# One weight load issued earlier at the start, one addition moved from VectorE to ScalarE and GpSimd at the end

## The chip, the cores and the metric

The kernel runs on one core of a Trainium2 chip. The metric is device time in microseconds (us), from launch to the last byte of the output; lower is better. A profile of one execution stands beside it, and its span is the time between the first and the last instruction that the profiler saw.

## What is computed

Four sequences of 768 rows with 8 heads of width 64 go through a linear attention with decay, and the result, laid out as 3072 rows of 512, through a two-layer network with a residual. In the reference, cut to what matters (blocks of 64 rows, `lam` one decay factor per head):

```
intra = (qb @ kb.T * Dmask) @ vb                 # Dmask: lam ** (i - j), lower triangle
inter = (qb * lam_pow) @ kv_state
out   = intra + inter
kv_state = lam ** 64 * kv_state + (kb * rev_pow).T @ vb
...
xn = (x - mean) / sqrt(var + 1e-6) * g_ln        # x: 512 wide, all heads of a row
y  = x + relu(xn @ w_ch1) @ w_ch2                # w_ch1: 512 x 2048, w_ch2: 2048 x 512
```

## The kernel before, in words

The rows are cut into 12 windows of 256 rows, numbered u = 0 to 11; window u belongs to sequence u mod 4, and in a window each of the 128 partitions holds two rows. For every window the three inputs q, k and v are loaded (f32, 512 KB each), brought to bf16 with powers of the decay multiplied in (`in_k`, `in_q`, `in_v`), k and q are transposed, and TensorE does the scores, the products with v, the state, and the part that comes from the state. The result is normalised (`norm`), transposed again (`to_xT`) and passed through the network (`mlp(g)`, one group g for each window). The first product of the network takes W1 in four pieces, `w1[0]` to `w1[3]`, the second W2 in four pieces. Windows 0 and 1 take the second product as it stands (`m2`), the groups from 4 on do it with seven half-size products (`m2w`, P1 to P7) that are combined by `evict`.

Nothing is left to a scheduler. The program is one list of calls, each engine executes its own instructions in the order in which they stand in the list, and an engine whose next instruction waits stands still with all that is behind it. Five queues matter here.

- **SP** issues the loads of q, k and v. Window 0 is loaded in two halves of four heads (`load_window(0, parts=2)`, line 126, in the order k, q, k, q, v, v), then k and q of window 1 (lines 756 and 757); v of window 1 is issued late, behind a memset on VectorE (lines 785 and 786).
- **GpSimd (POOL)** makes the constants, casts the second half of window 0's k (`in_k(0, nc.gpsimd, HB)`, line 768), issues the pieces of W1 and W2 (`load_w1`, `load_w2`; these transfers change f32 to bf16 or f16 on the way), multiplies v (`in_v`), and takes half of window 1's q (line 977).
- **VectorE (DVE)** takes the first half of k and all of q of window 0, later the other half of window 1's q (line 978), the masks and the normalisations.
- **ScalarE (ACT)** computes the powers of the decay (`lam_q`, line 185), copies out the transposes, casts all of window 1's k (line 972), and applies the activation behind the first product.
- **TensorE (PE)** follows the list: transposes of window 1's k, the transposes of window 0's first half of normalised rows, the transposes of window 1's q (lines 999 and 1000), the first tile of the first product (`m1a.tile(0, 0)`, line 1001, needs `w1[0]`), the scores of window 1, the second tile (`m1a.tile(0, 1)`, line 1010), and then the product with `w1[1]` (line 1011).

A transfer is held back with `behind(x)`: GpSimd copies one column of x into a spare tile, so that it waits for x, and all that it issues later waits with it.

```
743  def behind(tile_ap):
745      nc.gpsimd.tensor_copy(seen_p, tile_ap)
975  behind(st[1]["kq"][:, 0, 0, 0, 0, 0:1])
976  load_w1(1)
979  behind(w1[0][:, 0, 0:1])
980  load_w1(2)
981  load_w1(3)
```

In this way `w1[1]` is issued when ScalarE has cast window 1's k, and the last two pieces when `w1[0]` has landed.

At the end of the last group the seven products come in the order P1, P2, P7, P5, P6, P4, P3. P1 and P6 go to PSUM tile a, P2 to b, P7 and P4 to c, P5 and P3 to d. `evict(i)` adds a finished product to the rows of x, times the factor of the row. For P1 and P7 ScalarE multiplies and GpSimd adds; for the others VectorE does both in one instruction (`scaled`, line 595). P6 is used twice: for both halves of the second 128 rows (one instruction of 128x512) and for the second half of the first 128 rows (one of 128x256). As soon as a quarter of the output is complete, `last_rows` has it stored, half by SP and half by ScalarE (line 636).

Of the kernel before, what the change touches and what calls it, by code (L numbers as in the profile page):

```python
# [11 lines left out]
ALU = mybir.AluOpType  # L12
ACT = mybir.ActivationFunctionType
# [4 lines left out]
def kernel(  # L18
# [11 lines left out]
    nc = tc.nc  # L30
# [4 lines left out]
    NU = B * S // W  # L35
# [80 lines left out]
    def load_w1(c):  # L116
        nc.gpsimd.dma_start(w1[c], moe_w_ch1[:, c * W1C:(c + 1) * W1C].rearrange("(k p) f -> p k f", p=128))
# [66 lines left out]
    lam_q = const.tile([128, H, 2], F32)  # L184
# [20 lines left out]
    def part(a, dst, hs):  # L205

        return dst[:, a, hs.start // 2:hs.stop // 2].rearrange("p a j e d -> p a e j d")
# [3 lines left out]
    def in_k(u, eng, hs=ALL):  # L211
        src = qkv_in[u]["k"][:, hs].rearrange("p (a e) j d -> p a e j d", e=2)
        dst = part(0, st[u]["kq"], hs)
        for j in range(2):
            (eng.copy if eng is nc.scalar else eng.tensor_copy)(dst[:, :, :, j], src[:, :, :, j])

    def in_q(u, eng, hs=ALL):
        src = qkv_in[u]["q"][:, hs].rearrange("p (a e) j d -> p a e j d", e=2)
        dst = part(1, st[u]["kq"], hs)
        if u < LB:  # L220
            lq = lam_q[:, hs, :].rearrange("p (a e) j -> p a e j", e=2)
        else:
            lq = lam_p[:, 0:1, hs].rearrange("p j (a e) -> p a e j", e=2).to_broadcast([128, (hs.stop - hs.start) // 2, 2, 2])
        n = (hs.stop - hs.start) // 2
        for j in range(2):
            eng.tensor_tensor(dst[:, :, :, j], src[:, :, :, j],
                              lq[:, :, :, j:j + 1].to_broadcast([128, n, 2, D]), op=ALU.mult)
# [304 lines left out]
    def mlp(g):  # L532
# [36 lines left out]
        pr = {}  # L569
# [15 lines left out]
        ev = {}  # L585

        def evict(i):
            u = g
            x, rstd = x_keep[u]
            w = DM // 2  # L590
            r = [rstd[:, ab:ab + 1] for ab in range(2)]
            xq = [[x[:, ab, z * w:(z + 1) * w] for z in range(2)] for ab in range(2)]

            def scaled(out, in0, ab, in1):
                nc.vector.scalar_tensor_tensor(out, in0=in0, scalar=r[ab], in1=in1, op0=ALU.mult, op1=ALU.add)  # L595

            def tmp(name):
                ev[name] = wk.tile([128, w], F32, tag="ev_" + name, bufs=1, name="ev_" + name)
                return ev[name]

            if i == "P1":
                o_of[u] = x
            o = o_of[u]
            oq = [[o[:, ab, z * w:(z + 1) * w] for z in range(2)] for ab in range(2)]
            if i == "P1":
                nc.scalar.activation(tmp("u1"), pr["a"], ACT.Identity, scale=r[0])  # L606
                nc.gpsimd.tensor_tensor(oq[0][0], ev["u1"], xq[0][0], op=ALU.add)  # L607
            elif i == "P2":
                scaled(oq[0][0], pr["b"], 0, oq[0][0])
                if u == NU - 1:  # L610
                    for j in range(2):
                        nc.sync.dma_start(rows_of(u)[j][:, 0, 0:w], o[half[j], 0, 0:w])
            elif i == "P7":
                nc.scalar.activation(tmp("p7"), pr["c"], ACT.Identity, scale=r[1])
                nc.gpsimd.tensor_tensor(xq[1][1], ev["p7"], xq[1][1], op=ALU.add)  # L615
            elif i == "P5":
                scaled(xq[1][1], pr["d"], 1, xq[1][1])
            elif i == "P6":
                scaled(o[:, 1].rearrange("p (z w) -> p z w", z=2), pr["a"][:, None, :].to_broadcast([128, 2, w]), 1,
                       x[:, 1].rearrange("p (z w) -> p z w", z=2))  # L620
                last_rows(1, 1)
                scaled(oq[0][1], pr["a"], 0, xq[0][1])
            elif i == "P4":
                scaled(oq[1][0], pr["c"], 1, oq[1][0])
                last_rows(1, 0)
            elif i == "P3":
                scaled(oq[0][1], pr["d"], 0, oq[0][1])
                last_rows(0, 1)

        def last_rows(ab, z):  # L630
            u = g
            if u < NU - 1:
                return
            sl = slice(z * (DM // 2), (z + 1) * (DM // 2))
            for j, eng in enumerate((nc.sync, nc.scalar)):
                eng.dma_start(rows_of(u)[j][:, ab, sl], o_of[u][half[j], ab, sl])
# [7 lines left out]
        def m2w(n):  # L644
            for q, r in order[7 * n:7 * n + 7]:
                i, bank, first = products[q]
                product(i, bank, [r], first and r == 0)
                if r == 7:
                    evict(i)
# [44 lines left out]
    def rows_of(u):  # L694

        cc, b = divmod(u, B)
        order = "(c p j) d -> j p c d" if u < LB else "(j c p) d -> j p c d"
        return out[b, cc * W:(cc + 1) * W, :].rearrange(order, c=2, j=2)
# [43 lines left out]
    def behind(tile_ap):  # L742

        seen_p = wk.tile([128, 1], F32, tag="seen_p", name="seen_p")
        nc.gpsimd.tensor_copy(seen_p, tile_ap)
# [19 lines left out]
    nc.vector.tensor_copy(e_p[:, 0:1], io_p)  # L765
    nc.vector.tensor_scalar(e_p[:, 1:2], e_p[:, 0:1], -1.0, None, op0=ALU.mult)
    in_q(0, nc.vector, HA)
    in_k(0, nc.gpsimd, HB)
    load_w1(0)
    in_q(0, nc.vector, HB)  # L770
    transpose_pe(0, 1, (0, 1))
    transpose_pe(0, 0, (2, 3), nc.vector)
# [618 lines left out]
```

## Time and profile before

| | |
|---|---|
| median of three runs | 208.27 us (207.52 to 208.6) |
| the profiled execution's own time | 207.48 us |
| its span | 205.7 us |
| PE busy | 195.9 us, 95% |
| DVE, ACT, POOL busy | 133.4, 122.0, 83.9 us |
| granted TensorE clock | 1.0 |

The profiled execution is 0.79 us below the median, and 1.78 us of its own time lie outside the span. PE is busy nearly throughout; the profile's own page warns that a busy PE is not PE at its peak, but here it means that little idle time is left to win: the idle time of PE lies at the start, before 21 us, and after its last product at the end.

### The profile page before, as it was taken

To read this page: it belongs to the slowest core of one execution; us is meant where nothing else is said; L and a number is where in the kernel's file an instruction comes from. 1 tells how busy PE (TensorE), PEld (TensorE's weight loads), DVE (VectorE), ACT (ScalarE), POOL (GpSimd) and SP (SyncE) were. 2 spreads that over 40 slices of the span, in tenths; PEclk is the share of its full clock that TensorE was granted. 3 is DMA by queue.
4 is the path that set the end of the run, shared out by engine and by line. 5 is a ranking of instruction groups with operands and counts; after the bars stand their busy time and mean duration, and the time that the engine had idled before them with its cause. 6 is when DMAs were issued, how large, how long until landed. Compare 5 with 4: busy or idle time off the path is not lost.

```text
span 205.7 us, 7488 instructions
## 1 busy us (share of the span) xinstructions
PE 195.9 (95%) x3223; PEld 157.8 (77%) x3223; DVE 133.4 (65%) x277; ACT 122.0 (59%) x281; POOL 83.9 (41%) x117
## 2 busy tenths in 40 slices
PE   1997999999999999999999999999999999999992
PEld 0485798545784686489889888888888888988881
DVE  3588352626766458777889774857877947865253
ACT  3787678535357468166575775585586565652630
POOL 5557039317656341464273261772273202002020
PEclk9999999999999999999999999999999999999999
DMA  3999999999899998999799999887988020178404
GB/s 105 301 255 203 179 281 192 198 293 277 194 268 252 217 183 190 170 256 213 165 201 134 220 213 135 207 169 128 234 133 183 4 51 3 26 131 273 139 7 97
DMA packets 91011, 36.41 MB, mean 177 GB/s; under 512 B 65121, under 2 KB 88161, under 8 KB 90978
## 3 DMA queue, kind: packets, MB, share of 16 engines
q1 hardware_dynamic: 86368, 31.53, 74.9%
q0 software_dynamic: 4224, 4.19, 12.7%
q8 instruction: 25, 0.41, 0.9%
q10 hardware_dynamic: 386, 0.20, 0.4%
q14 instruction: 8, 0.07, 0.1%
HBM read 27.27 MB, written 6.29 MB: 163 GB/s over the span
## 4 chain that ended last, share of the span: by engine, by line
PE 85%; DMA 6%; DVE 2%; ACT 2%; SPq 1%; issue 1%; POOL 0%; POOLq 0%; DVEq 0%
PE pm L547 34%; PE pm L684 14%; PE pm1t L658 6%; PE pwd L582 6%; PE pwa L582 6%; PE pwc L582 6%; DMA w<-in_moe_w_ch_dram 4%; PE pwb L582 3%; DMA qin<-in_q_dram 3%; PE po L449 2%; PE po L436 2%; DVE x L595 1%; PE po L423 1%; PE sc L370 1%; PE sc L279 1%; PE pk L324 1%
## 5 line engine op out<-in xcount | busy, mean ns | idle before, releaser
L547 PE MATMUL pm<-xT,w 128*128 128x256 bf16 x640 | 73.9, 273 | 0.4 <-DMA w<-in_moe_w_ch_dram 0.4
L547 PEld LDWEIGHTS <-w 128*128 128x128 bf16 x640 | 61.2, 98 | 8.7 <-DMA w<-in_moe_w_ch_dram 0.5
L550 ACT ACTIVATE hT<-pm 128x512 f16<-128x512 f32 x80 | 47.1, 597 | 28.7 <-PE pm L547 28.5
L684 PE MATMUL pm<-w,hT 128*128 128x512 f16 x128 | 29.8, 380 | 0.0
L582 PEld LDWEIGHTS <-hs 128*128 128x128 f16 x256 | 24.9, 98 | 2.9
L607 POOL TENSOR_TENSOR x<-ev_u,x 128x256 f32<-128x256 f32 x8 | 5.9, 743 | 48.8 <-ACT ev_u L606 37.4
L330 POOL TENSOR_TENSOR Sn<-Stmp,lam_s 128x256 bf16<-128x256 f32 x16 | 9.8, 616 | 33.0 <-DVE Stmp L408 17.9
L565 DVE TENSOR_TENSOR hs<-hT 128x1024 f16<-128x1024 f16 x16 | 12.7, 795 | 15.8 <-ACT hT L550 14.5
L684 PEld LDWEIGHTS <-hT 128*128 128x128 f16 x128 | 11.8, 98 | 12.4
L582 PEld LDWEIGHTS <-hT 128*128 128x128 f16 x192 | 18.7, 98 | 2.1
L658 PE MATMUL pm1t<-xT,w 128*128 128x128 bf16 x256 | 15.6, 219 | 1.0 <-DMA w<-in_moe_w_ch_dram 0.7
L477 DVE SCALAR_TENSOR_TENSOR xc<-po,nmean,g_row 128x512 bf16<-128x512 f32 x18 | 13.0, 745 | 5.0 <-ACT nmean L476 4.9
L658 PEld LDWEIGHTS <-w 128*128 128x128 bf16 x256 | 14.8, 98 | 1.5 <-DMA w<-in_moe_w_ch_dram 0.8
L475 ACT ACTIVATE x<-po 128x512 f32<-128x512 f32 x18 | 10.6, 590 | 7.8 <-PE po L449 4.5
L242 POOL TENSOR_TENSOR vb<-vin,lam_v 128x1024 bf16<-128x1024 f32 (+1 forms) x7 | 11.6, 1659 | 4.8 <-DMA vin<-in_v_dram 4.7
L520 ACT ACTIVATE sq<-x,nmean 128x512 bf16<-128x512 f32 x18 | 12.9, 719 | 0.3
L242 POOL TENSOR_TENSOR vb<-vin,lam_p 128x1024 bf16<-128x1024 f32 x6 | 11.4, 1896 | 3.1 <-ACT hT L550 1.9
L289 DVE TENSOR_TENSOR mA<-sc,keep 128x512 bf16<-128x512 f32 x14 | 9.0, 682 | 4.9 <-PE sc L279 4.9
L661 ACT ACTIVATE hT<-pm1t 128x512 f16<-128x512 f32 x16 | 9.6, 598 | 4.4 <-PE pm1t L658 4.3
L595 DVE SCALAR_TENSOR_TENSOR x<-pwd,rstd,x 128x256 f32<-128x256 f32 x16 | 7.7, 481 | 3.4 <-POOL x L615 3.4
L595 DVE SCALAR_TENSOR_TENSOR x<-pwa,rstd,x 128x512 f32<-128x512 f32 (+1 forms) x16 | 9.1, 612 | 0.8
L582 PE MATMUL pwa<-w,hT 128*128 128x256 f16 x64 | 9.6, 273 | 0.0
(137 smaller groups left out, 318.0 us busy)
## 6 DMA issues: line engine op xcount, KB each, us to landing
out_dram<-x SPq DMA_DIRECT2D x22, 256.0 KB, 4.0
w<-in_moe_w_ch_dram POOLq DMA_DIRECT2D x8, 512.0 KB, 8.0
kin<-in_k_dram SPq DMA_DIRECT2D x14, 256.0 KB, 5.2
qin<-in_q_dram SPq DMA_DIRECT2D x14, 256.0 KB, 4.2
vin<-in_v_dram SPq DMA_DIRECT2D x14, 256.0 KB, 5.3
kin<-in_k_dram SPq DMA_DIRECT2D x5, 512.0 KB, 6.2
qin<-in_q_dram SPq DMA_DIRECT2D x5, 512.0 KB, 7.0
vin<-in_v_dram SPq DMA_DIRECT2D x5, 512.0 KB, 6.1
```

Source lines behind the costliest of these rows:

```text
L242: eng.tensor_tensor(st[u]["vb"][:, hs], qkv_in[u]["v"][:, hs], lv.to_broadcast([128, n, 2, D]), op=ALU.mult)
L330: eng.tensor_tensor(dst, src, lam_s[:, :, None].to_broadcast([128, NP, D]), op=ALU.mult)
L475: nc.scalar.activation(x, po, ACT.Copy, accum_out=sm)
L477: nc.vector.scalar_tensor_tensor(xc, in0=po, scalar=nm, in1=g_row, op0=ALU.add, op1=ALU.mult)
L520: nc.scalar.activation(sq, s["x"][:, ab], ACT.Square, bias=s["nmean"][:, ab:ab + 1], accum_out=ss[:, ab:ab + 1])
L547: nc.tensor.matmul(pm[:, b, :], lhsT=w1[n // W2K][:, kk, (n % W2K) * 128:(n % W2K + 1) * 128], rhs=xT_of[g][:, kk, 0:N], start=(b == 0 and ...
L550: nc.scalar.activation(hT[:, u * NB:(u + 1) * NB, 0:N], pm, ACT.Relu)
L565: nc.vector.tensor_tensor(s13, b[:, :, 1:2, :].to_broadcast([128, n, 2, 128]), b[:, :, 0:4:3, :], op=ALU.subtract)
L582: nc.tensor.matmul(pr[bank], lhsT=lhs(r), rhs=rhs, start=(first and r == 0), stop=(r == KB // 2 - 1), skip_group_check=True)
L595: nc.vector.scalar_tensor_tensor(out, in0=in0, scalar=r[ab], in1=in1, op0=ALU.mult, op1=ALU.add)
L658: nc.tensor.matmul(pm[:, b, :], lhsT=w1[c][:, kk, b * 128:(b + 1) * 128], rhs=xT_of[g][:, kk, i * 128:(i + 1) * 128], start=(b == 0 and kk ...
L684: nc.tensor.matmul(acc[i], lhsT=hT[:, kk, i * 128:(i + 1) * 128], rhs=w2[kk // W2K][:, kk % W2K, :], start=(kk == 0), stop=(kk == KB - 1))
```

## The change

Two edits. At the start, `load_w1(0)` moves from behind GpSimd's cast of the second half of window 0's k (called the first pair in the change's description) to ahead of it, and a `behind` on the first column of `lam_q` is put before it, so that GpSimd first waits for ScalarE's computation of `lam_q`. The casts follow after the issue of the transfer. At the end, in the last group alone, the 128x256 half of P6 is no longer added by VectorE: ScalarE multiplies it into the tile `ev_u1`, which P1 has used before, and GpSimd adds it to x.

```diff
@@ evict @@
             elif i == "P6":
+                if u == NU - 1:
+                    nc.scalar.activation(tmp("u1"), pr["a"], ACT.Identity, scale=r[0])
+                    nc.gpsimd.tensor_tensor(oq[0][1], ev["u1"], xq[0][1], op=ALU.add)
                 scaled(o[:, 1].rearrange("p (z w) -> p z w", z=2), pr["a"][:, None, :].to_broadcast([128, 2, w]), 1,
                        x[:, 1].rearrange("p (z w) -> p z w", z=2))
                 last_rows(1, 1)
-                scaled(oq[0][1], pr["a"], 0, xq[0][1])
+                if u < NU - 1:
+                    scaled(oq[0][1], pr["a"], 0, xq[0][1])
@@ the start @@
     in_q(0, nc.vector, HA)
+    behind(lam_q[:, 0, 0:1])
+    load_w1(0)
     in_k(0, nc.gpsimd, HB)
-    load_w1(0)
     in_q(0, nc.vector, HB)
```

## The prediction

> **What bounds the kernel now.** I read the list of who waited for whom on TensorE first, because it is 95% busy; over the whole execution it holds five lines, of which these matter here:
>
> ```profile
> PE pm1t L658 <- DMA w<-in_moe_w_ch_dram: 0.7, 1, 0.7
> PE pm L547 <- DMA w<-in_moe_w_ch_dram: 0.4, 1, 0.4
> ```
>
> PE waits 0.7 us for `w1[0]` at 17.0 us and 0.4 us for `w1[1]` at 20.83 us. From there to the last product no wait of PE is listed, so a shift at 20.83 us moves the end by as much. The chain of waits between 11 and 21 us says what sets that moment:
>
> ```profile
> 11.80 0.93 ACT Sn L349 x4
> 12.73 0.52 ACT kq L215
> 13.24 0.05 issue
> 13.30 0.12 POOL seen_p L745
> 13.42 7.37 DMA w<-in_moe_w_ch_dram
> 20.79 0.05 issue
> 20.83 0.28 PE pm L547
> ```
>
> ScalarE casts window 1's k, GpSimd sees it and issues `w1[1]`, which lands at 20.79. The moved piece is not in this chain. Next I asked for DMA queues by stretch. From 8 to 11.5 us, from 13 to 14, and from 38 to 41.5 (one line each, all that moved):
>
> ```profile
> q1 hardware_dynamic: 2024, 1.02, 114.2%
> ...
> q0 software_dynamic: 205, 0.21, 125.6%
> ...
> q0 software_dynamic: 688, 0.69, 119.8%
> ```
>
> q1 holds SP's loads, q0 GpSimd's. `w1[0]` is issued from 8.01 to 8.95 but moves nothing until 11.5: k and q of window 1, issued at 5.36 to 6.07 and 6.11 to 7.82, go first. At 38 us it is the other way: k and q of window 3, issued at 38.06 and 38.47, move nothing until the earlier pieces of W2 are through. So the engines serve transfers in the order of arrival, and they are full. Last, VectorE's order and POOL's, from the timeline:
>
> ```profile
> 14.25 1.39 POOL L226 TENSOR_TENSOR kq<-qin,lam_q 128x256 bf16<-128x256 f32 x2
> 14.67 1.25 DVE L226 TENSOR_TENSOR kq<-qin,lam_q 128x256 bf16<-128x256 f32 x2
> 15.85 0.68 DVE L482 BATCH_NORM_STATS2 stats<-po 128x6 f32<-128x512 f32 x1
> ```
>
> Neither waits for window 1's q, which took 7.1 us from its issue at 6.11 and landed at 13.2: slack of 1.05 us on POOL and 1.5 us on DVE.
>
> [...] the trace shows no mixing in the stretches above, so I go by order of arrival[...]. [...] the pair at 14.67, beside POOL's, took 1.25 us, the same pair for window 0 at 8.03 took 0.76.
>
> **The start, on GpSimd.** Added is one copy (0.19 for each of the three casts at L745, 0.42 for its f32 copy). `lam_q` is ready at 6.04 + 0.30 = 6.34; the transfer's issue follows 0.12 after the copy starts, as at 13.30, so it runs from about 6.5 to 7.4 (0.94, as now). The two casts (0.90) then run from 7.45 to 8.35 instead of 7.16 to 8.06. Behind them stand PE's transposes of that half; but the ones after them wait for VectorE's q, ready at 8.79, and end at 9.35. Four transposes from 8.4 take about 0.4 and are just in time. VectorE's copy (0.41, now at 8.71) ends by 9.4, before the scores at 10.02. POOL's `in_v(0)` starts near 8.4 instead of 9.04: no gain, since the state that uses it waits for ScalarE (busy to 11.77). [...] I price all this at 0, with 0 to 0.4 for the range.
>
> **The start, in the DMA line.** Now the issue of `w1[0]` begins after that of window 1's q (6.11 to 7.82) has ended; changed, it runs from 6.5 to 7.4, inside it. Part of q then stands behind 512 KB of weights. The bytes are the same, so the group k, q, `w1[0]` is through when it is now, only with q last. `w1[0]` moved 0.19 MB from 11.5 to 13, 0.21 to 14, 0.12 to 15.5: all of it; but the release of its waiter is at 17.0, 1.5 us after nearly everything has moved. Window 1's q inherits a landing between 15.5 (no such tail) and 17.0 (all of it). I take 16.7, for the tail belongs to whatever is last in the group.
>
> What is late then, if q lands at 17.0: VectorE's pair 1.25 to 18.25, and behind it, in its order, the normalisation of window 0's second half, whose products are ready: 1.75 from the pair's end to its last result (now 15.92 to 17.67), to 20.0. POOL's pair to 18.4; PE's transposes end 0.69 after it (15.64 to 16.33 now), 19.1. PE is in order: `m1a.tile(0, 0)` 1.07 to 20.15, scores 0.42 to 20.55, transposes of the normalised rows to 20.8 (0.40), ScalarE's copy 0.04 + 0.58 to 21.4, `m1a.tile(0, 1)` 0.05 + 1.05 to 22.5. The product with `w1[1]` starts at 22.5 instead of 20.83: 1.7 lost. Landing at 15.3 would lose nothing, each tenth beyond it costs a tenth. At 16.7: **+1.4**. POOL's next `behind` and with it `w1[2]` and `w1[3]` come 1.4 later too, as late as their products.
>
> `w1[0]` itself comes earlier, but PE can't use it before the transposes of that q.
>
> **The end.** VectorE loses one addition, 0.39 of its time (201.00 to 201.39 between starts; row mean 474 ns). Added are an ACT of 128x256 from PSUM (473 ns, as L606) and a POOL addition (726 ns, as L607). P6's product is finished at 200.09: ACT to about 200.65, POOL to 201.45. P3, which needs the sum, can't start before PE's last product at 201.83, so 0.4 of cover hides it; without cover it would cost what POOL is late. VectorE's P3 starts at 201.87 today, so it is PE-bound already and gains nothing. What moves is P4, and with it the stores in ScalarE's queue:
>
> ```profile
> 201.11 0.55 ACTq L636 DMA_DIRECT2D out_dram<-x  x1
> ...
> 201.90 1.40 ACTq L636 DMA_DIRECT2D out_dram<-x  x2
> ...
> 202.45 0.55 SPq L636 DMA_DIRECT2D out_dram<-x  x1
> ```
>
> ScalarE's second store runs 201.90 to 202.53 and holds up its third, which needs only P3 (done 202.35; SP's third starts at 202.45). With P4 done at 201.5 the second starts at 201.7 and the third at 202.45 instead of 202.63: **-0.18**. The new ACT instruction stands ahead of the first store but is done by 200.65. Bounds: -0.2 and +0.1, if two engines reading one PSUM tile slow each other, which no row shows.
>
> **Sum.** 1.4 - 0.18 = +1.2 on the profiled span of 205.7, so 206.9, and its own time 207.48 becomes 208.7. The median shown is 0.79 above that execution: 208.27 + 1.2 = **209.5**.
>
> **Rivals.** (a) *q keeps its place*: SP's loads are all in the line before GpSimd's transfer is ready, which now takes until 11.5 to show any traffic. Then the start does nothing and the time is 208.27 - 0.18 = 208.1. For it: the line has never been seen to mix. Against: the issue lies inside that of q. It decides if q lands before 15.3. (b) *The weights gain*: q stays in time and the slow tail at 15.5 to 17 now hits SP's loads alone, so that `w1[0]` and then `w1[1]` land earlier. PE could take the first tile when its transposes end at 16.33 and not 17.0, finish the second at 19.8, and start with `w1[1]` there if it has landed: up to 1.0 + 0.18 less, 207.1. For it: 0.52 MB had moved by 15.5. Against: the bytes ahead of `w1[1]` are unchanged and its issue at 13.42 is too. (c) *q late without the tail*: landing at 16.0, +0.7 - 0.18, 208.8. (d) *k late too*: `w1[0]` gets in ahead of part of window 1's k, ScalarE's cast slips from 12.60, and all its transposes with it: 1.8 to 2.0 worse, 210.2. That the edit does nothing at all is excluded by its own instructions; that it moves no data is (a).
>
> **Chances and range.** q late with the tail 38 in 100 (likeliest; own range 209.0 to 210.0), (c) 13, (a) 20, (b) 24, of which 17 gain over 0.5%, (d) 5. About 0.5%, 1.04 us, is what a measurement of this kernel can tell from no change. Slower: 36 of the first and all of (d), 41. Faster: 17. Same: the remaining 42, of several mechanisms. Range: from (b)'s end at 207.2 to just under (d), 210.1.
>
> **What would show it.** Right: POOL's issue of `w1[0]` near 6.5; `w1[0]` landing before 16; VectorE's L226 of window 1 starting after 16 with a wait for DMA qin ahead of it; the first L547 near 22.2 with PE waiting on ScalarE or POOL, not on weights; at the end ACTq's third store near 202.45 on the old clock. Wrong: L226 still at 14.67 (then a), or the first L547 before 20.5 (then b).

## The result and the profile after

The changed kernel is slower: 210.24 us median (209.45 to 211.5, 4 runs) beside 207.9 us (207.44 to 208.6, 4 runs) for the kernel before, a ratio of 1.0124 with a 95% interval of 1.0086 to 1.0162. The profiled execution took 210.54 us and its span is 208.8 us, 3.1 more than before. In every ratio of this document, runs more than 1.5% above the fastest of their kernel are left out; the counts of runs include them. Line numbers behind the two edits are four or five higher (line 658 is now 662, `evict`'s stores are at 640).

**The first reading is the page's busy time.**

```profile
PE 198.4 (95%) x3223; PEld 160.1 (77%) x3223; DVE 136.9 (66%) x276; ACT 122.5 (59%) x282; POOL 84.4 (40%) x119
```

TensorE has the same 3223 matmuls as before, yet it is busy for 198.4 us instead of 195.9. Most of the lost time is therefore no waiting at all: it is counted as work. The list of TensorE's waits over the whole execution says the same from the other side (waited for, us in total, times, longest):

```profile
PE g_all L180 <- DMA g_one<-in_moe_g_ln_dram: 4.2, 1, 4.2
PE tp L250 <- POOL kq L226: 1.2, 2, 0.8
```

Both waits for weights (0.7 and 0.4 us before) are gone, and a wait for window 1's q has come: 1.2 us where 0.2 stood. The list alone would say that nothing was lost.

**The transfers.** The DMA view of the stretch from 5 to 8 us lists what was issued there, with KB each and the us from issue to landing:

```profile
kin<-in_k_dram SPq DMA_DIRECT2D x1, 512.0 KB, 5.9
qin<-in_q_dram SPq DMA_DIRECT2D x1, 512.0 KB, 9.7
w<-in_moe_w_ch_dram POOLq DMA_DIRECT2D x1, 512.0 KB, 8.1
```

Window 1's q took 7.1 us before, now 9.7; its issue starts at 6.16, so it lands near 15.85 instead of 13.2. `w1[0]`, issued from 6.63 to 7.57, lands near 14.7 instead of 17.0. k is not later (5.9 us, before 6.2). From 10 to 11.5 us both queues move data (0.20 MB of weights, 0.12 MB of SP's), where before SP's queue moved alone until 11.5. The timeline shows who waited for q:

```profile
15.84 1.18 DVE L226 TENSOR_TENSOR kq<-qin,lam_q 128x256 bf16<-128x256 f32 x2 [0.94 <-DMA qin<-in_q_dram]
15.90 1.60 POOL L226 TENSOR_TENSOR kq<-qin,lam_q 128x256 bf16<-128x256 f32 x2 [1.51 <-DMA qin<-in_q_dram]
```

They had started at 14.67 and 14.25, without a wait.

**TensorE between 14 and 24 us**, from its timeline (start, us, what, how many, and in brackets the idle time ahead of it), first before the change, then after it:

```profile
17.00 1.07 PE L658 MATMUL pm1t<-xT,w 128*128 128x128 bf16 x16 [0.67 <-DMA w<-in_moe_w_ch_dram]
...
20.83 1.05 PE L547 MATMUL pm<-xT,w 128*128 128x256 bf16 x8 [0.37 <-DMA w<-in_moe_w_ch_dram]
```

```profile
15.64 0.40 PE L306 MATMUL unread<-warm 128*128 128x128 bf16 x2
16.80 0.29 PE L250 MATMUL tp<-ident,kq 128*128 128x128 bf16 x1 [0.76 <-POOL kq L226]
...
18.27 1.91 PE L662 MATMUL pm1t<-xT,w 128*128 128x128 bf16 x16
...
21.97 1.66 PE L662 MATMUL pm1t<-xT,w 128*128 128x128 bf16 x16
23.46 0.71 PE L547 MATMUL pm<-xT,w 128*128 128x256 bf16 x5
```

The two tiles of the first product took 1.07 and 1.05 us before; they now take 1.91 and 1.66. The first product with `w1[1]` starts at 23.46 instead of 20.83: 2.63 us late, most of the 3.1. The groups by shape from 16 to 23.5 us show that it isn't one kind of instruction (busy us, mean ns of one | idle ahead):

```profile
L662 PE MATMUL pm1t<-xT,w 128*128 128x128 bf16 x32 | 3.6, 301 | 0.1
...
L279 PE MATMUL sc<-kqT 64*64 64x128 bf16 x16 | 0.6, 311 | 0.0
```

Before, these two stood at 219 and 222 ns: every matmul there takes about 90 ns longer. Matmuls overlap, so what counts is how far apart they start: 0.107 us in the slow tiles, 0.056 in the fast ones, which makes 0.84 us for the sixteen of the first tile. It is the rate of the first microseconds, which lasts longer now: the eight transposes of k at 13.87 us took 1.06 us, as much as sixteen matmuls of the same shape at the later rate.

The page's row of the granted clock shows 9 in all these slices, as before, and the table ahead of the prediction gives 1.0: both count a stretch without an entry as full. The trace's own record of that clock has its first entry, at full clock, at 14.71 us in the kernel before and at 23.27 in the changed kernel, and in both it is there that matmuls go from 314 to 219 ns. I call this moment the rise. In the kernel before it came ahead of the first tile, in the changed kernel only at the end of the second.

**The end**, from the timeline of the last microseconds, VectorE's last two additions before the change and then the changed kernel:

```profile
201.39 0.47 DVE L595 SCALAR_TENSOR_TENSOR x<-pwc,rstd,x 128x256 f32<-128x256 f32 x1
201.87 0.48 DVE L595 SCALAR_TENSOR_TENSOR x<-pwd,rstd,x 128x256 f32<-128x256 f32 x1
```

```profile
203.07 0.47 ACT L620 ACTIVATE ev_u<-pwa,rstd 128x256 f32<-128x256 f32 x1 [1.56 <-PE pwa L582]
203.57 0.75 DVE L595 SCALAR_TENSOR_TENSOR x<-pwa,rstd,x 128x512 f32<-128x512 f32 x1 [0.75 <-ACT ev_u L620]
...
204.43 0.48 DVE L595 SCALAR_TENSOR_TENSOR x<-pwc,rstd,x 128x256 f32<-128x256 f32 x1
204.83 0.47 DVE L595 SCALAR_TENSOR_TENSOR x<-pwd,rstd,x 128x256 f32<-128x256 f32 x1
```

VectorE's 128x512 waits for ScalarE's instruction, though neither uses what the other writes; both read P6's product in PSUM tile a. PE's last product ends at 203.39 + 1.04 = 204.43. Counted from there, P4's addition starts at 0.00 (before: 201.39 − 201.83 = −0.44) and P3's at +0.40 (before +0.04). From PE's end to the span's end it is 208.8 − 204.43 = 4.37 us, before 205.7 − 201.83 = 3.87: 0.50 lost. So 2.63 + 0.50 = 3.13, the whole of the 3.1.

### The profile page after: what moved, and what is told of

The parts are those of the page before. It is cut to its first block, busy times and chain, and to the rows that moved or that the text cites. A ratio compares the mean times of both kernels' runs of the same rounds, so it can differ in the third digit from the quotient of the medians.

```text
span 208.8 us, 7491 instructions
## 1 busy us (share of the span) xinstructions
PE 198.4 (95%) x3223; PEld 160.1 (77%) x3223; DVE 136.9 (66%) x276; ACT 122.5 (59%) x282; POOL 84.4 (40%) x119
## 4 chain that ended last, share of the span: by engine, by line
PE 88%; ACT 3%; POOL 2%; DMA 2%; issue 2%; DVE 1%; DVEq 0%; POOLq 0%
PE pm L547 34%; PE pm L688 14%; PE pm1t L662 8%; PE pwd L582 6%; PE pwa L582 6%; PE pwc L582 6%; PE pwb L582 3%; DMA lam_b<-in_lam_dram 2%; PE po L436 2%; PE po L449 2%; PE tp L250 1%; PE sc L279 1%; PE xt L510 1%; PE sc L370 1%; PE po L423 1%
## 5 line engine op out<-in xcount | busy, mean ns | idle before, releaser
L547 PE MATMUL pm<-xT,w 128*128 128x256 bf16 x640 | 73.9, 273 | 0.0
L547 PEld LDWEIGHTS <-w 128*128 128x128 bf16 x640 | 61.2, 98 | 8.2 <-DVE Smid L405 0.3
L688 PEld LDWEIGHTS <-hT 128*128 128x128 f16 x128 | 11.7, 98 | 12.4
L662 PE MATMUL pm1t<-xT,w 128*128 128x128 bf16 x256 | 17.1, 229 | 0.2
L662 PEld LDWEIGHTS <-w 128*128 128x128 bf16 x256 | 16.3, 103 | 0.6 <-issue 0.4
```

The costliest lines, as they stand in the source:

```text
L547: nc.tensor.matmul(pm[:, b, :], lhsT=w1[n // W2K][:, kk, (n % W2K) * 128:(n % W2K + 1) * 128], rhs=xT_of[g][:, kk, 0:N], start=(b == 0 and ...
L662: nc.tensor.matmul(pm[:, b, :], lhsT=w1[c][:, kk, b * 128:(b + 1) * 128], rhs=xT_of[g][:, kk, i * 128:(i + 1) * 128], start=(b == 0 and kk ...
L688: nc.tensor.matmul(acc[i], lhsT=hT[:, kk, i * 128:(i + 1) * 128], rhs=w2[kk // W2K][:, kk % W2K, :], start=(kk == 0), stop=(kk == KB - 1))
```

## The experiments

Two theories stood for the start. *A: the order in the DMA line*: q stands behind the weights, comes late, and TensorE, which has not reached its full rate by then, stays slow because it stood idle. *B: GpSimd*: the issue and the wait ahead of the casts disturb what follows. For the end: *C: the shared PSUM tile* orders the two readers; *D: the added work* takes time from VectorE. Each profile is read by two numbers: when the first product with `w1[1]` starts (20.83 us before), and how long the span lasts after PE's end (3.87 before).

### Each edit alone

The start edit alone takes the second hunk of the diff (the issue ahead of the cast), the end edit alone the first.

```diff
@@ start edit alone @@
+    behind(lam_q[:, 0, 0:1])
+    load_w1(0)
     in_k(0, nc.gpsimd, HB)
-    load_w1(0)
```

> The edit at the start alone; the end as before. Theory A (window 1's q stands behind the weights, lands about 15.9 us instead of 13.2, and PE, left idle, runs its first tiles at about 314 ns a matmul instead of 219): nearly the whole loss, +1.9 to +2.3 us (ratio 1.009 to 1.011), first product with w1[1] at 22 to 23.5 us. Theory B (the loss is mostly at the end): at most +0.6 us.

> The edit at the end alone; the start as before. Theory A: +0.4 to +0.5 us (ratio 1.002), because VectorE's P6 now stands behind ScalarE's reading of the same PSUM tile, and P4 and P3 behind it; first product with w1[1] near 20.8 us. The step as predicted: -0.18 us (0.999), P6 beginning beside ScalarE's instruction. Theory B: +1.5 us or more.

The start edit alone: 209.28 us (14 runs), ratio 1.0061 (1.0034 to 1.0088). Its profile has the first product with `w1[1]` at 23.64, the two tiles at 1.91 and 1.49 us, and after PE's end 208.5 − 204.64 = 3.9, as before. The end edit alone: 208.37 us (14 runs), ratio 1.0009 (0.9981 to 1.0037), so the clock shows nothing; in its profile the span lasts 206.8 − 202.40 = 4.4 us after PE's end and P3's addition starts 0.39 after it. Each loss stays with its own edit. The clock tells of the start's loss; the end's rests on the profiles. The two ratios add to 1.007, and only the edges of the intervals meet the 1.0124 of both.

### The order in the line alone

The kernel before, with window 1's q issued by SP only when GpSimd has issued `w1[0]` (a memset of q's first column by GpSimd, behind `load_w1(0)`, holds SP). GpSimd's casts stay ahead of the weights, as before.

```diff
     load_in(1, "k", nc.sync)
-    load_in(1, "q", nc.sync)
...
     in_k(0, nc.gpsimd, HB)
     load_w1(0)
+    nc.gpsimd.memset(qkv_in[1]["q"][:, 0, 0:1], 0.0)
+    load_in(1, "q", nc.sync)
```

> The kernel before with w1[0] issued where it was, but window 1's q issued after it (SP waits for a memset on GpSimd that follows the weights' issue). GpSimd's casts and the early weights are as before; only the order in the DMA line is turned. If the order is the cause: q lands at 15.5 to 16.5 us and the loss is that of the start alone within 0.5 us (1.008 to 1.012). If the earlier issue of the weights or GpSimd's own delay is the cause: as before, within 0.3%.

Measured: 209.14 us (22 runs), ratio 1.0066 (1.0046 to 1.0086), which is the start edit's loss. TensorE's timeline:

```profile
16.59 0.29 PE L250 MATMUL tp<-ident,kq 128*128 128x128 bf16 x1 [0.75 <-POOL kq L226]
...
18.07 1.91 PE L658 MATMUL pm1t<-xT,w 128*128 128x128 bf16 x16
...
22.45 1.04 PE L547 MATMUL pm<-xT,w 128*128 128x256 bf16 x8
```

It has the same late q (issued only at 9.08, it lands near 15.6; VectorE's pair starts at 15.64 behind a wait of 0.92), the same idle time of TensorE, the same slow first tile, and the first product with `w1[1]` at 22.45, 1.62 later than before. Nothing on GpSimd was reordered against its casts, and its profiled execution, 209.16, is close to its median. So a q behind the weights is enough for the start edit's loss; what the slow rate comes from is asked below.

### Later weights, with q in its place

The start edit with the gate moved: `w1[0]` waits for VectorE's first half of window 0's q instead of `lam_q`, and so is issued from 7.77 to 8.71.

```diff
-    behind(lam_q[:, 0, 0:1])
+    behind(st[0]["kq"][:, 1, 0, 1, 0, 0:1])
     load_w1(0)
     in_k(0, nc.gpsimd, HB)
```

> The edit at the start alone, but GpSimd waits for VectorE's first half of window 0's q (done at 7.5 us) and not for lam_q (6.3 us): the weights are issued about 1 us later, near 7.6 us, and are still ahead of the casts, which slip to 8.6 to 9.5 us. If q's place in the DMA line is the cause, q is ahead again by then: it lands at 13 to 14 us, VectorE's pair starts without a wait or with one under 0.3 us, and what is left of the loss is the lateness of the casts, 0.3 to 0.6 us (1.002 to 1.003). If the early issue harms in another way, the loss stays at 1.006.

Measured: 209.84 us (9 runs), ratio 1.0091 (1.0062 to 1.0121). q took 7.1 us again, as before, and nobody waits for it: that half came as expected. The loss didn't. The timeline of GpSimd and TensorE:

```profile
8.72 0.98 POOL L215 CAST kq<-kin 128x256 bf16<-128x256 f32 x2
9.42 1.27 PE L250 MATMUL tp<-ident,kq 128*128 128x128 bf16 x8 [1.27 <-POOL kq L215]
```

The casts are now 1.1 us later than in the changed kernel (7.58), and TensorE stands still for 1.27 us at once. ScalarE's cast of window 1's k and with it the issue of `w1[1]` move to 14.76 (13.57 in the changed kernel). In its profiled execution, the shortest of the nine, the first product with `w1[1]` starts at 22.23. So B's mechanism exists too; the prediction's 8.35 for the end of the casts (in the changed kernel they end at 8.32) was just early enough.

### TensorE kept busy while it waits for q

Here is the test of "late" against "slow". The start edit, with more matmuls of line 306, whose result nobody reads (a filler), ahead of the transposes of q: 14 instead of 2, and in a further kernel 22. The third is the kernel before with 14.

```diff
-    fill_pe(2, "sc", True)
+    fill_pe(14, "sc", True)
     norm(0, 1, early=True)
```

> The edit at the start alone, and 12 more unread 128x128 matmuls on PE just ahead of the transposes of window 1's q (about 1.3 us of work at 0.11 us each), in the stretch in which PE stood idle. Nothing else changes: q is as late as in the run of the start alone. If PE's slow matmuls come from its idling: the tiles run at about 219 ns, and the loss falls to about +1.0 us (1.005). If they are chance, or if lateness is the whole loss: no better than the start alone, 1.009 to 1.011.

> As the run with 12 unread matmuls, but with 20, so that PE isn't idle at all while q is late. If PE's slow matmuls come from the idle stretch: the change to 219 ns a matmul comes before 18 us, the first product with w1[1] starts at 21.2 to 22 us, and the ratio is at or below 1.005. If the fast rate comes by chance or the loss is lateness alone: 1.006 as without them.

> The kernel before with the 12 unread matmuls of the earlier run. q is on time here and PE has little idle time to fill. If the rate of PE in this stretch is mostly decided by idle time: no change, within 0.2%. If such matmuls bring the fast rate sooner by themselves: 0.997 or less, and then they are an improvement of their own.

The start edit with 14: q is as late as in the changed kernel (VectorE's pair at 15.85). Groups by shape, 16 to 21.2 us:

```profile
L658 PE MATMUL pm1t<-xT,w 128*128 128x128 bf16 x31 | 2.1, 219 | 0.3 <-ACT xT L511 0.3
```

TensorE has its full rate, and the first product with `w1[1]` starts at 21.26, 0.43 later than before; with 22 it starts at 21.25. So at full rate a late q is worth 0.43, and in the profiled execution of the changed kernel the slow matmuls were worth the other 23.46 − 21.26 = 2.20. Lateness costs so little because of what it covers: both tiles start 0.96 later than before, but the 0.4 us that TensorE stood waiting for `w1[1]` is no longer waited.

But it was not the filler that brought this rate. Here are the filler's own lines: 14 with the start edit, 22 with it, and 14 in the kernel before.

```profile
15.70 1.08 PE L306 MATMUL unread<-warm 128*128 128x128 bf16 x14
...
15.12 1.40 PE L306 MATMUL unread<-warm 128*128 128x128 bf16 x22
...
15.83 1.68 PE L306 MATMUL unread<-warm 128*128 128x128 bf16 x14
```

The clock's first entry stands at 16.00, 11.92 and 19.13 us in these three. With 22 the rise was there 3.2 us before the filler began. With 14 it came 0.3 us after its start, when TensorE of the changed kernel was still busy too (its two matmuls from 15.64 end at 16.04). In the kernel before, the filler ran slow to its end. These profiles show what a late q costs once the rate is full; that a filler brings the rise isn't shown.

The times agree with that. With 14: 209.08 us (22 runs), ratio 1.0058 (1.0033 to 1.0083), no better than without the filler; the profiled run, 208.11, with its early rise, is among its fastest. With 22, 210.12 us (6 runs), ratio 1.0107 (1.0056 to 1.0158): the first product with `w1[1]` at 21.25, so this part is as good, and then 187.55 us to the end of the span instead of 184.9. One line of its list of TensorE's waits stands for half of that, at 64.1 us:

```profile
PE po L449 <- issue: 1.3, 1, 1.3
```

TensorE stood there with nothing that the profile shows to wait for; the cause stays open. The kernel before with 14: 208.0 us, ratio 1.0015 (0.9996 to 1.0034): nothing gained; in its profile the filler delays the first tile to 18.15 us. No run here shows that matmuls whose result nobody reads pay.

### Is the slow rate chance?

The start edit alone, profiled once more.

> The changed start alone, profiled once more. There the first product with the second piece of W1 started at 23.64 us, about 1.0 from the late q and 1.7 from matmuls of 128x128 at 314 instead of 219 ns. If PE's slow matmuls after the late q are a rule, it starts at 22.8 or later again, with at least one of the two tiles of line 658 at 290 ns or more. If they are chance from one execution to the next, it can start at 21.6 to 22.0 with both tiles at 219 ns and q landing late all the same.

```profile
17.60 0.29 PE L250 MATMUL tp<-ident,kq 128*128 128x128 bf16 x1 [1.35 <-POOL kq L226]
...
19.07 1.91 PE L658 MATMUL pm1t<-xT,w 128*128 128x128 bf16 x16
```

Its first product with `w1[1]` starts at 24.08, in a run of 210.77 us; both tiles are slow (1.91 and 1.47). Over all profiles it divides cleanly. With q late and no added filler (the changed kernel, this kernel twice, the order in the line alone) the first tile took 1.91 us each time, and in three of the four the second was slow as well. With q on time, in seven profiles, the first took 1.07 to 1.82 and the second always 1.05. The rise divides in the same way: 14.71 to 19.45 us in the seven with q on time, 20.48, 23.27, 23.27 and 23.69 in the four with q late and no filler. With q on time a late rise costs little, for TensorE has waits for weights to lose (0.7 and 0.4 us in the kernel before): with VectorE's additions reordered (the last run below) the rise came at 17.57 and the first tile took 1.61, and the first product with `w1[1]` still started at 20.44.

What brings the rise isn't shown. From one profile to the next its moment moves by several microseconds, and in the four profiles with a late q and no filler it lay behind all of those with q on time. At the transposes of q TensorE had waited 1.2 us in the changed kernel, 1.5 and 1.8 in the start edit alone and 1.2 with the order in the line alone; in the seven with q on time it waited 0.2 there at most. Such a wait can't be all that matters: the seven, with next to no wait there, spread over 4.74 us themselves. That the wait for q puts the rise off, and not something else that comes with a late q, is an estimate of mine from these figures; no run with a late q took the idle time away ahead of the rise.

### The end: who waits for whom, and why

First the end edit alone, with VectorE's 128x512 written ahead of ScalarE's and GpSimd's instructions:

```diff
             elif i == "P6":
-                if u == NU - 1:
-                    nc.scalar.activation(tmp("u1"), pr["a"], ACT.Identity, scale=r[0])
-                    nc.gpsimd.tensor_tensor(oq[0][1], ev["u1"], xq[0][1], op=ALU.add)
                 scaled(o[:, 1].rearrange("p (z w) -> p z w", z=2), pr["a"][:, None, :].to_broadcast([128, 2, w]), 1,
                        x[:, 1].rearrange("p (z w) -> p z w", z=2))
                 last_rows(1, 1)
+                if u == NU - 1:
+                    nc.scalar.activation(tmp("u1"), pr["a"], ACT.Identity, scale=r[0])
+                    nc.gpsimd.tensor_tensor(oq[0][1], ev["u1"], xq[0][1], op=ALU.add)
```

> The edit at the end alone, with VectorE's 128x512 instruction written ahead of ScalarE's, not behind it. If two readers of one PSUM tile are put in the order in which they are written: VectorE starts P6 as before the change, ScalarE begins only when VectorE is done (0.75 us), GpSimd ends 1.2 us after that, and P3 starts about 0.6 us later than in the kernel before, against PE's last product; ratio 1.003. If they may read together: P3 starts within 0.1 us of PE's last product, ratio 0.999.

Measured: 208.56 us (20 runs), ratio 1.0037 (1.0015 to 1.0059). The timeline of the end:

```profile
202.50 0.47 ACT L623 ACTIVATE ev_u<-pwa,rstd 128x256 f32<-128x256 f32 x1 [2.86 <-DVE x L595]
...
203.81 0.48 DVE L595 SCALAR_TENSOR_TENSOR x<-pwd,rstd,x 128x256 f32<-128x256 f32 x1 [1.41 <-POOL x L624]
```

Now ScalarE waits for VectorE, and for its own first store at 201.85 to 202.40 besides. P3's addition starts 1.24 us after PE's last product (202.57) behind GpSimd's sum. The order of the two readers is that in which they are written, so the wait isn't a matter of one engine being slow. (The 1.24 isn't all turn-taking: 0.55 of it is the store that stands ahead of ScalarE's instruction.)

Then the end edit alone, where ScalarE reads the finished product b instead of a; a quarter of the last rows gets another product's values, and all instructions and sizes stay.

```diff
-                    nc.scalar.activation(tmp("u1"), pr["a"], ACT.Identity, scale=r[0])
+                    nc.scalar.activation(tmp("u1"), pr["b"], ACT.Identity, scale=r[0])
```

> The changed end alone, but ScalarE's added instruction reads the finished product b instead of a, so that one quarter of the last rows gets another product's values; all instructions and their sizes stay. If VectorE's wait of 0.74 us for ScalarE comes from both reading product a, it goes: VectorE's 128x512 starts as in the kernel before, P3's addition within 0.1 us of PE's last product (0.39 in the changed end alone), and the span after PE's end falls from 4.4 to 3.7, below the kernel before's 3.87 by the 0.18 that I had forecast. If it comes from something else, such as ScalarE or GpSimd taking time from VectorE, the 4.4 stays. Ratio to the kernel before 0.997 to 1.001 in the first case, 1.001 to 1.004 in the second.

Measured: 207.63 us (12 runs), ratio 0.9994 (0.9967 to 1.0022). The timeline:

```profile
200.28 0.75 DVE L595 SCALAR_TENSOR_TENSOR x<-pwa,rstd,x 128x512 f32<-128x512 f32 x1
...
201.14 0.48 DVE L595 SCALAR_TENSOR_TENSOR x<-pwc,rstd,x 128x256 f32<-128x256 f32 x1
201.89 0.48 DVE L595 SCALAR_TENSOR_TENSOR x<-pwd,rstd,x 128x256 f32<-128x256 f32 x1 [0.27 <-PE pwd L582]
```

The wait is gone, VectorE now waits for TensorE, and P3's addition starts 0.11 after PE's end at 201.78. ScalarE has the same work, and in turn waited 0.36 us for VectorE's addition of P2, the other reader of b. Theory C holds: the loss was the shared tile. (ScalarE reads b at 199.22, before P6 is finished; so no run shows the two engines reading two tiles at the same moment.) The gain is another matter: 205.6 − 201.78 = 3.82, only 0.05 below the kernel before, where 0.18 was expected.

The last run asks for that 0.18 with no other engine in it: the kernel before, with VectorE's second addition of P6 moved behind P4's in the last group.

```diff
                 last_rows(1, 1)
-                scaled(oq[0][1], pr["a"], 0, xq[0][1])
+                if u < NU - 1:
+                    scaled(oq[0][1], pr["a"], 0, xq[0][1])
             elif i == "P4":
                 scaled(oq[1][0], pr["c"], 1, oq[1][0])
                 last_rows(1, 0)
+                if u == NU - 1:
+                    scaled(oq[0][1], pr["a"], 0, xq[0][1])
```

> The kernel before with one edit: in the last group VectorE's second addition from product a comes after P4's instead of ahead of it, all on VectorE. My term of 0.18 said that P4 0.39 us earlier lets ScalarE's second store go earlier and with it the third. If right: P4 starts about 0.39 us earlier against PE's end than in the kernel before, P3 stays within 0.1 us of PE's last product, and the span after PE's end is 3.70 instead of 3.87; ratio 0.999, which the clock can't tell from 1. If the stores' end does not follow ScalarE's queue, the span after PE's end stays 3.85 to 3.95.

Measured: 207.73 us (22 runs), ratio 0.9997 (0.9976 to 1.0017). The expectation missed: PE's last product ends at 201.69, and from there it is 4.0 us to the end of the span. Two lines of the timeline, ScalarE's second store and VectorE's addition of P3:

```profile
201.62 0.78 ACTq L639 DMA_DIRECT2D out_dram<-x  x1
...
202.03 0.48 DVE L595 SCALAR_TENSOR_TENSOR x<-pwd,rstd,x 128x256 f32<-128x256 f32 x1
```

P4's addition starts 0.64 us ahead of PE's end (201.05), before 0.44: 0.20 earlier, where 0.39 was expected. ScalarE's second store starts earlier with it: 0.07 ahead of PE's end, before it was 0.07 behind it (201.90 against 201.83). But P3's addition starts 0.34 after PE's end, because the moved addition is still running when PE finishes, and both third stores wait for it: they start at 202.54, it ends at 202.51. In the run with product b P3 isn't late, and there the second store itself takes the gain: it starts 0.07 ahead of PE's end but lasts 0.78 us instead of 0.63, so that the third starts 0.80 after PE's end (202.58), before 0.79 (202.62). Freeing ScalarE's queue earlier gave next to nothing.

## Why the prediction was right or wrong

**Right: that the place to read was the start, and that q pays.** Of the signs named for it these came: POOL's issue at 6.63, `w1[0]` landing at 14.7, window 1's pair on VectorE behind a wait for q, and no weight wait ahead of line 547. The pair started at 15.84, just short of the "after 16"; the first L547 came at 23.46 and not near 22.2, and the third store didn't come earlier. GpSimd's casts cost next to nothing, as priced: TensorE's scores start at 9.43 instead of 9.28. Rival (a) is out, and (b) too: the weights are early and can't be used. Rival (d) is out, for k was not later. What follows the first product with `w1[1]` passes to the end in full, as the first step said: from there to the end of the span it is 184.87 us before and 184.86 to 185.02 in the other kernels with the old end and no filler.

**Wrong in "What is late then": TensorE's rate.** The step took every duration of TensorE from the kernel before (1.07 for a tile, 0.42 for the scores) and moved them. In the changed kernel the two tiles took 1.91 and 1.66, the scores 0.64, because the clock rose at 23.27 us and not at 14.71. I counted TensorE's wait for q as time lost once and took the rate behind it as given.

**Mis-sized in "The start, in the DMA line": the landing.** I took 16.7; q landed near 15.85, between rival (c)'s 16.0 and the 15.5 named as the lower end: of the tail of 1.5 us that q was to inherit, 0.35 came. The rule beside it, that each tenth beyond 15.3 costs a tenth, gives 0.55 for 15.85, and the two kernels with the start edit and a filler measured 0.43 and 0.42 for lateness at the full rate. In place of the +1.4 stand 0.43 of lateness and, in the profiled execution, 2.20 of slow matmuls. By the ratio the start edit costs 0.61% of 207.6, 1.3 us: near the +1.4 on the clock, for a reason half of which I hadn't seen. The two errors had opposite signs, so the nearness is luck. The first profiled execution of the start edit is the longest of its 14 runs (210.25), the second longer still, so the 2.20 is more than the usual loss.

**Wrong in "The end": the term of −0.18 is +0.50.** The step had ScalarE's new instruction finish by 200.65 beside VectorE's, and bounded two engines reading one PSUM tile by −0.2 and +0.1. In fact they took turns: VectorE waits 0.75 us, P4's addition 0.44 later against PE's end and P3's 0.36. "P3 is PE-bound already and gains nothing" held only as long as VectorE had time to spare. The wait goes with the tile: 0.75 us with tile a shared, none with tile b. The other half of the step, that an earlier P4 lets the stores end 0.18 earlier, failed by itself: where the wait was taken away, P4 came 0.20 earlier and not 0.39, and the end 0.05.

**The sum.** In the medians +2.3 instead of +1.2; in the profiles 2.63 + 0.50 instead of 1.4 − 0.18. 210.24 lies just above the range's 210.1. Its upper end was drawn for a k that comes late too; what was missing were two costs, the slow rate and the turn-taking.

**What stays open**: what exactly makes the clock rise, and so whether any filler could bring it in time; why the two edits together measured 1.0124 where the two alone add up to 1.007; the 1.3 us at 64.1 us with 22 fillers; and why ScalarE's second store takes 0.78 instead of 0.63 us when it starts earlier.

No version here is shown to beat the kernel before.

## What to carry to other kernels

Here `w1[0]`, issued at 6.63 us instead of 8.01, came into the stretch in which another queue was issuing q (from 6.16), and q landed near 15.85 instead of 13.2: before a transfer is issued earlier, name the one that it may displace and who reads it next. When an engine will stand idle where it didn't, don't take its rate afterwards from the old profile (here 0.107 us between starts of matmuls instead of 0.056); busy time that grows with an unchanged count of instructions is the sign of it. Before a filler is credited with the rate, look at how fast the filler's own matmuls ran. Before work is moved to another engine, look whether both engines will read the same PSUM tile, and count them one after the other, as here, where VectorE waited 0.75 us for ScalarE.

## What the runs showed of the hardware that I had not expected

- The page's granted clock reads full from the first slice on, but the trace's record of it begins only at the rise, between 11.92 and 23.69 us in thirteen profiles; in the kernel before and in the changed kernel matmuls of 128x128 go there from 314 to 219 ns, and from 0.107 to 0.056 us between starts. In the four profiles in which TensorE waited 1.2 to 1.8 us for q, and no filler was added, the rise came latest, at 20.48 to 23.69 us.
- The weights and q, issued in overlapping stretches (6.63 to 7.57, and from 6.16), moved side by side: 0.13 MB of weights and 0.06 of q from 11.5 to 12.4 us, when k had landed and v wasn't issued. In the kernel before, SP's queue moved alone from 8 to 11.5 us (1.02 MB), from which the prediction took its order of arrival; from 11.5 to 12.1 both queues moved data there too (0.13 MB of SP's, 0.03 of weights).
- Two readers of one PSUM tile on ScalarE and VectorE went one after the other in the order in which they were written, at a price of 0.75 us for VectorE in the one order; in the other P3's addition came 1.24 us after PE's last product, 0.55 of it a store.
